# Loading the state by plain DMA in three parts, the last one gated, and batch 0 by plain DMA and casts on the engines, with a reordered instruction table

## The chip, the cores and the metric

The kernel runs on one core of a Trainium2 chip. Its inputs and outputs lie in HBM in f32. The metric is the time of one execution on the device in microseconds; smaller is better. Every experiment ran on the same chip as runs of the kernel before, in the same rounds; the sets of experiments ran on different chips, so that across sets the ratios to the kernel before are the safer comparison. A run counts as slow when it is over 1.5% above the fastest of the same kernel; the verdicts use the other runs, called fast, alone.

## The reference, cut to what matters

```python
# x: (8 batches, 8 heads, 512 tokens, 64), state: (8, 8, 32, 64)
a     = softmax(x @ state^T / 8)          # tokens read the state
xread = a @ state
a2    = softmax(state @ x^T / 8)          # the state reads the tokens
sread = a2 @ x
y     = concat([xread, sread], axis=2)    # (8, 8, 544, 64) -> (8, 544, 512)
# mixer: wq = y @ w_q, wk = y @ w_k, W = wq . wk^T / 8
out   = relu(W^T @ y) @ w_out             # (8, 544, 512)
```

The eight batches are independent of each other. All of them need the state; the weights and the state are small (1.25 MB with w_out, 0.5 MB), x and the output are 8.4 and 8.9 MB.

## The kernel before

The program is a list of steps in the variable ORDER, such as `xT0.1.t`: the step, its batch, and the engine that does it (t TensorE, v VectorE, a ScalarE, p GpSimd). Each engine executes its own steps strictly in this order. The first steps bring the data in:

```python
    for t in range(2):                     # w_q on SyncE's queue, w_k on ScalarE's
        for r in range(2):
            eng = nc.sync if t == 0 else nc.scalar
            eng.dma_start(out=w_f[64 * r : 64 * r + 64, :, t, :], in_=wsrc[t][r])
    ...
    def load(n, b, e):
        if n == "ist":                     # the whole state, cast to bf16 by GpSimd's DMA
            nc.gpsimd.dma_start(out=st_in, in_=state.rearrange(...))
            make_identity(nc, ident)
        elif n == "iwo":                   # w_out, cast on the way
            nc.gpsimd.dma_start(out=w_o, in_=moe_w_out.rearrange("(k p) e -> p k e", p=128))
        elif n[2] == "0":                  # batch 0 in two halves, cast on the way
            ...
        else:                              # batches 1 to 7, cast on the way
            nc.gpsimd.dma_start(out=x_bf[b], in_=xsrc(b, 0, H))
    ...
    def st_tr(n, b, e):                    # 64 transposes of 64x64: state to stT
    def st_back(n, b, e):                  # 16 transposes back: stT to st_bf (head layout)
    def stbd_blk(n, b, e):                 # block-diagonal state of batches 0 to 2, on GpSimd
    def stbd_dma(n, b, e):                 # the same of batches 3 to 7, by four DMAs
    ...
    def pt_mm(n, b, e):                    # scores: x^T times stT
    def srd(n, b, e):                      # 64 small matmuls of 32 columns: a2 @ x
    def mixs_mm(n, b, e):                  # 4 matmuls: the state rows of the mixer
    def fin_mm(n, b, e):                   # 4 matmuls of 512 columns: times w_out
```

All loads of x and w_out go through one queue, GpSimd's, one after the other; I call them the batch stream.

The softmax here doesn't subtract the row's maximum and nothing guards it: scores larger than these inputs give would overflow.

## Time and profile before

| | before |
|---|---|
| time, first three runs | 98.1 us median (95.94 to 99.06) |
| span of the profiled run | 95.1 us |
| TensorE busy | 81.4 us (86%) |
| TensorE's waits for a batch | 4.7 us, three times, longest 2.3 |
| last batch landed | at about 32 us |

### The profile page before, as it was taken

To read this page: it belongs to the slowest core of one execution; us is meant where nothing else is said; L and a number is where in the kernel's file an instruction comes from. 1 tells how busy PE (TensorE), PEld (TensorE's weight loads), DVE (VectorE), ACT (ScalarE), POOL (GpSimd) and SP (SyncE) were. 2 spreads that over 40 slices of the span, in tenths; PEclk is the share of its full clock that TensorE was granted. 3 is DMA by queue.
4 is the path that set the end of the run, shared out by engine and by line. 5 is a ranking of instruction groups with operands and counts; after the bars stand their busy time and mean duration, and the time that the engine had idled before them with its cause. 6 is when DMAs were issued, how large, how long until landed. Compare 5 with 4: busy or idle time off the path is not lost.

```text
span 95.1 us, 3128 instructions
## 1 busy us (share of the span) xinstructions
PE 81.4 (86%) x1376; PEld 54.3 (57%) x1376; DVE 57.3 (60%) x108; ACT 50.5 (53%) x78; POOL 38.5 (40%) x50
## 2 busy tenths in 40 slices
PE   5852898918999999999999999999999999999300
PEld 4542796806897855865875678478655544344000
DVE  3946267833385959926899689196942647637000
ACT  0507467970738994525762679468496430542400
POOL 5999609999402900290008999006113000000000
PEclk9995559995569999999999999999999999999995
DMA  0999999999999130545410253016302634762990
GB/s 6 177 153 158 194 200 205 196 200 196 198 198 145 28 52 29 234 184 215 171 62 7 110 214 127 0 45 258 148 10 58 266 124 186 324 259 48 341 352 22
DMA packets 14245, 14.51 MB, mean 153 GB/s; under 512 B 2904, under 2 KB 11608, under 8 KB 14232
## 3 DMA queue, kind: packets, MB, share of 16 engines
q0 software_dynamic: 8944, 4.98, 38.4%
q1 hardware_dynamic: 4312, 8.42, 23.8%
q10 hardware_dynamic: 976, 0.92, 2.8%
q8 instruction: 10, 0.16, 0.6%
q14 instruction: 3, 0.02, 0.1%
HBM read 10.22 MB, written 8.91 MB: 201 GB/s over the span
## 4 chain that ended last, share of the span: by engine, by line
PE 68%; DMA 16%; POOL 5%; ACT 2%; issue 2%; ACTq 1%; POOLq 0%
PE fin_ps L537 28%; DMA x_bf<-in_x_dram 16%; PE xT_ps L245 5%; PE mix_ps L503 5%; PE at_ps L321 4%; PE wq_ps L397 3%; PE pt_ps L263 3%; PE wk_ps L435 3%; PE g_ps L451 3%; PE v_ps L467 2%; PE srd_ps L334 2%; PE fins_ps L537 2%; ACT ost L128 2%; POOL x_bf L153 2%; PE v_ps L476 2%
## 5 line engine op out<-in xcount | busy, mean ns | idle before, releaser
L537 PE MATMUL fin_ps<-w_o,rmix 128*128 128x512 bf16 x128 | 30.2, 379 | 0.0
L308 POOL TENSOR_TENSOR A<-E,rinv 128x1024 bf16<-128x1024 bf16 (+1 forms) x9 | 15.4, 1720 | 22.9 <-DVE rinv L302 15.1
L537 PEld LDWEIGHTS <-rmix 128*128 128x128 bf16 x128 | 11.5, 98 | 12.0 <-issue 0.4
L245 PE MATMUL xT_ps<-ident,x_bf 128*128 128x128 bf16 x128 | 11.2, 245 | 4.7 <-DMA x_bf<-in_x_dram 4.7
L130 DVE COPY ost<-fin_ps 128x1024 f32<-128x1024 f32 (+1 forms) x9 | 10.4, 1164 | 6.0 <-PE fin_ps L537 4.5
L371 POOL TENSOR_TENSOR sbd<-srn,mask 128x256 bf16<-128x256 bf16 x16 | 9.4, 614 | 9.4 <-DVE srn L361 9.4
L128 ACT COPY ost<-fin_ps 128x1024 f32<-128x1024 f32 (+1 forms) x9 | 7.8, 871 | 9.3 <-PE fin_ps L537 8.7
L134 ACT ACTIVATE rmix<-mix_ps 128x1024 bf16<-128x1024 f32 x11 | 11.3, 1028 | 2.7 <-PE mix_ps L503 2.6
L279 ACT ACTIVATE E<-pt_ps 128x512 bf16<-128x512 f32 x16 | 9.5, 600 | 5.5 <-PE pt_ps L263 5.5
L245 PEld LDWEIGHTS <-x_bf 128*128 128x128 bf16 x128 | 8.9, 111 | 5.5 <-DMA x_bf<-in_x_dram 5.4
L294 DVE TENSOR_REDUCE rsum<-E 128x16 f32<-128x512 bf16 x16 | 10.6, 670 | 0.0
L128 ACT COPY xT<-xT_ps 128x1024 bf16<-128x1024 bf16 x8 | 8.2, 1019 | 2.3 <-PE xT_ps L245 2.3
L130 DVE COPY xT<-xT_ps 128x1024 bf16<-128x1024 bf16 x8 | 5.4, 681 | 4.3 <-PE xT_ps L245 4.2
L263 PE MATMUL pt_ps<-stT,xT 128*128 128x64 bf16 x128 | 7.1, 205 | 0.0
L130 DVE COPY AT<-at_ps 128x1024 bf16<-128x1024 bf16 x6 | 4.1, 690 | 4.7 <-PE at_ps L321 4.7
L136 DVE TENSOR_SCALAR rmix<-mix_ps 128x1024 bf16<-128x1024 f32 x5 | 6.1, 1221 | 1.0 <-PE mix_ps L503 0.9
L263 PEld LDWEIGHTS <-xT 128*128 128x128 bf16 x128 | 5.9, 106 | 0.8
L153 POOL DMA_DIRECT2D x_bf<-in_x_dram x7 | 6.2, 917 | 0.4 <-DMA x_bf<-in_x_dram 0.4
L503 PE MATMUL mix_ps<-wq,V 64*128 64x256 bf16 x64 | 5.9, 273 | 0.0
L321 PE MATMUL at_ps<-ident,A 128*128 128x128 bf16 x64 | 5.5, 231 | 0.0
L321 PEld LDWEIGHTS <-A 128*128 128x128 bf16 x64 | 4.2, 104 | 0.7 <-issue 0.4
L128 ACT CAST wq<-wq_ps 128x288 bf16<-128x288 f32 x6 | 2.4, 400 | 4.0 <-PE wq_ps L406 4.0
(75 smaller groups left out, 116.0 us busy)
## 6 DMA issues: line engine op xcount, KB each, us to landing
out_dram<-ost SPq DMA_DIRECT2D x14, 512.0 KB, 2.8
x_bf<-in_x_dram POOLq DMA_DIRECT2D x7, 512.0 KB, 17.1
out_dram<-ost SPq DMA_DIRECT2D x3, 256.0 KB, 4.7
out_dram<-ost ACTq DMA_DIRECT2D x3, 256.0 KB, 4.2
x_bf<-in_x_dram POOLq DMA_DIRECT2D x2, 256.0 KB, 6.6
w_o<-in_moe_w_out_dram POOLq DMA_DIRECT2D x1, 512.0 KB, 13.3
st_in<-in_state_dram POOLq DMA_DIRECT2D x1, 256.0 KB, 4.3
stbd<-st_bf SPq DMA_DIRECT2D x4, 40.0 KB, 2.1
```

Of the source, the lines that this page charges most:

```text
L128: nc.scalar.copy(out=out, in_=in_)
L130: nc.vector.tensor_copy(out=out, in_=in_)
L134: nc.scalar.activation(out=out, in_=in_, func=AF.Relu)
L245: nc.tensor.transpose(out=ps[:, u, q, :], in_=x_bf[b][:, NP * r + q, 128 * u : 128 * u + 128], identity=ident,)
L263: nc.tensor.matmul(out=ps[:, 2 * u : 2 * u + 2, NS * q : NS * q + NS], lhsT=L[b][f"xTe{r}"][:, u, q, :], rhs=stT[:, b, :, NP * r + q, :], ...
L279: nc.scalar.activation(out=L[b]["E"][:, r].rearrange("p c q n -> p c (q n)"), in_=L[b][f"pt{r}"], func=AF.Exp, scale=float(scale),)
L294: nc.vector.reduce_sum(out=L[b]["rsum"][:, w], in_=L[b]["E"].rearrange("p r c q n -> p (r c q) n")[:, w], axis=AX.X,)
L308: eng.tensor_tensor(out=L[b]["A"].rearrange("p r c q n -> p (r c q) n")[:, w], in0=L[b]["E"].rearrange("p r c q n -> p (r c q) n")[:, w], ...
L321: nc.tensor.transpose(out=L[b]["at"][:, r, c, :], in_=L[b]["A"][:, r, c, :, :], identity=ident)
L371: nc.gpsimd.tensor_tensor(out=L[b]["sbd"][:, r], in0=L[b]["srn"][:, r : r + 1, :].to_broadcast((128, NP, D)), in1=mask[:, :, None].to_broa ...
L503: nc.tensor.matmul(out=ps[:, h, kk, :], lhsT=L[b]["V"][rows, 128 * k : 128 * k + 128], rhs=L[b]["wq"][rows, 0:SH], start=True, stop=True,)
L537: nc.tensor.matmul(out=ps, lhsT=lhs(k), rhs=w_o[:, k, :], start=(k == 0), stop=(k == KC - 1))
```

## The change

The intent is to start TensorE's real work sooner and to free GpSimd. The state comes by plain DMA, directly in the layout that st_bf needs, in parts for batch 0, batch 1, and batches 2 to 7. The third part is gated: it is issued only after a one-column fill on GpSimd that stands behind the first batch's normalising. Batch 0 comes by four plain DMAs on two queues and is cast by three engines. The block-diagonal state is made by eight small DMAs instead of GpSimd's products, and two zero fills move from VectorE to GpSimd. The table follows the expected landings.

```diff
+    def load_st(b0, b1):
+        nc.sync.dma_start(
+            out=st_f[:, b0:b1].rearrange("p b r d -> p (b r) d"), in_=st_src[:, 2 * b0 : 2 * b1]
+        )
+    load_st(0, 1)
+    for g in range(4):
+        eng = nc.sync if g % 2 == 0 else nc.scalar
+        eng.dma_start(out=x_f0[:, 2 * g : 2 * g + 2], in_=xsrc(0, 2 * g, 2 * g + 2))
+    load_st(1, 2)
...  (the four weight loads, all on SyncE now)
-        if n == "ist":  ...                      (whole state by casting DMA)
-        elif n[2] == "0":  ...                   (batch 0 by casting DMA)
+    def st_gate(n, g, e):
+        nc.gpsimd.memset(st_f[:, 2, 0, 0:1], 0.0)
+        load_st(2, B)
+    def st_cast(n, g, e):                        # f32 to bf16
+    def st_tr(n, g, e):                          # 32 transposes of 128x64 in four groups
-    def st_back ... stb_ev ... stbd_blk          (removed)
     def stbd_dma(n, g, e):                       # now for batches 0-1 and 2-7
...  (table, cut to the place that matters)
+swe.0.a xT0.1.t srn.0.v A1.0.p at0.0.t xTe0.1.v srT.0.t xT1.1.t srTe.0.a xTe1.1.a pt0.1.t gate.10.p
+ix4.0.p at1.0.t ate.0.v exp0.1.a pt1.1.t ix5.0.p stc.2.v wq.0.t exp1.1.a rs0.1.v stt.2.t ix6.0.p
```

## The prediction

> **What bounds the kernel now.** I read the page first: the busy shares, the 40 slices, and the chain that ended last.
>
> ```profile
> PE 81.4 (86%) x1376; PEld 54.3 (57%) x1376; DVE 57.3 (60%) x108; ACT 50.5 (53%) x78; POOL 38.5 (40%) x50
> ...
> PE   5852898918999999999999999999999999999300
> ...
> PEclk9995559995569999999999999999999999999995
> DMA  0999999999999130545410253016302634762990
> ...
> PE 68%; DMA 16%; POOL 5%; ACT 2%; issue 2%; ACTq 1%; POOLq 0%
> ```
>
> A slice is 2.38 us. From slice 10 on TensorE is full until the tail, so the last 65 us can only shrink with TensorE's work or its clock. The first ten slices are different: holes, and a granted clock of 0.5 in two stretches, while the DMA engines are full until slice 12. The chain in order of time names what holds the start:
>
> ```profile
> 4.04 1.76 POOL x_bf L153 x2
> 5.80 0.71 POOL w_o L147
> 6.51 15.25 DMA x_bf<-in_x_dram
> 21.80 1.04 PE xT_ps L245 x8
> ```
>
> The load of batch 3, issued at 6.51 us, lands at 21.8 us, and TensorE waits for it. The stretches (columns: stretch, length, busy time of PE, PEld, DVE, ACT, POOL, then clock, DMA share, GB/s) give the price:
>
> ```profile
> 8.84:14.30 5.46, 5.14 (x62) 4.70 (x63) 2.31 (x5) 3.12 (x4) 2.11 (x3) 0.51 1.42 190
> 14.30:21.80 7.50, 4.78 (x184) 3.79 (x181) 4.64 (x12) 5.83 (x9) 7.22 (x9) 0.95 1.38 200
> 21.80:28.30 6.50, 6.50 (x115) 5.55 (x116) 3.70 (x7) 2.50 (x5) 3.02 (x6) 0.53 1.46 198
> 28.30:89.00 60.70, 60.48 (x943) 36.97 (x939) 40.94 (x74) 35.95 (x56) 18.39 (x19) 1.00 0.39 135
> ```
>
> Up to 21.8 us TensorE idles 0.32 + 2.72 us; then, full, it runs at 0.53 for 6.5 us, which costs about 6.5 x 0.47 = 3.1 us; after that there is no hole. So three things are to be won: an earlier first transpose (now 8.84 us), the 2.3 us wait at 21.8, and the 3.1 us of slow clock that follow. The waits name the first as well:
>
> ```profile
> 8.84 0.77 PEld L245 LDWEIGHTS <-x_bf 128*128 128x128 bf16 x8 [2.15 <-DMA x_bf<-in_x_dram]
> 10.19 0.77 PEld L245 LDWEIGHTS <-x_bf 128*128 128x128 bf16 x8 [0.57 <-DMA x_bf<-in_x_dram]
> 21.80 0.77 PEld L245 LDWEIGHTS <-x_bf 128*128 128x128 bf16 x8 [2.48 <-DMA x_bf<-in_x_dram]
> ```
>
> **What the Trainium skill says.** "TensorE: Matmul & The Clock Gate", section "Why this matters for your kernels", asks for no TensorE gaps over about 3 us, or the clock halves. The trace agrees in kind, with a shorter gap: 2.3 us without work before 21.8 us, and 0.53 granted after it. "DMA: Bandwidth & Descriptors", section "Issuing engines are not separate DMA queues", says that DMAs of all issuers share the same 16 engines and interleave. The trace agrees: the first 64 KB weight load on ScalarE's queue moves its 272 packets between 2.0 and 3.0 us, the second, issued 0.7 us after the first, only between 4.0 and 5.5 us, with the state load on GpSimd's queue between them; landing goes from 3.2 to as much as 4.4 us. The same page, "Specifications", gives 512 B as the smallest piece at full rate. Here SyncE's queue took 9.7% of 16 engines over 6 us for 544 packets of mostly 256 B, 17 ns each; no run shows yet what they cost among larger ones.
>
> **The change, part by part.**
>
> Start. Now state, then batch 0, go through GpSimd's queue and land at 5.6, 8.84 and 10.2 us. In the new kernel SyncE issues a 64 KB state part, then batch 0 comes in four 256 KB pieces on two queues. Issues take 0.80 us on SyncE, so the first piece of SyncE leaves at about 1.55 us; with the 3.2 us of an early weight load and 0.6 us for its bytes it lands near 5.4 us. It is then cast by GpSimd, which first makes the identity (0.23 + 0.29 us) and fills two 128x2048 f32 tiles that VectorE filled before (1.76 and 1.12 us). No row shows such a fill on GpSimd; its fills of 1 and 128 columns take 0.10 and 0.23 us, 1.0 ns a column, so I estimate 2.1 us each. 1.25 + 0.6 + 4.2 = 6.05 us, and the cast is 0.61 us (as w_qk's): first transpose at 6.7 us, **2.1 us earlier**.
>
> TensorE's work. Gone: 64 small state transposes (1.2 us, beside a load) and 16 back transposes (1.03 us, on the path). New: 32 transposes of 64x128, four before the start; of the other 28, 24 stand at one place, an estimate of 1.0 us at full clock from the 19 ns apiece that 64 of half the width took. In total no gain worth naming.
>
> GpSimd. Six products for the diagonal state go (6 x 0.61 = 3.7 us), replaced by eight plain DMAs of 128 B rows; those of before landed 2.1 us after issue, long before v needs them. Beside the path, except that normalising batch 0 comes sooner: now A ends 18.13 - 8.84 = 9.3 us after the first transpose, of which w_qk's cast and two products (1.8 us), and parts of the back transpose (about 0.7 us), go. So about 6.8 us remain: 6.7 + 6.8 = 13.5 us.
>
> Batches. Batches 1, 2, 3 are issued from 6.7 us on, w_o after them. Landings stood 2.63 us apart late in the stream (24.4 to 32.3 us), about 2 us behind their bytes: 12, 15 and 17.6 us (now up to 12.9, 16.6, 21.8), w_o 20.5. But the queue starts 4 us later, so batches 4 to 7 gain about 0.5 us only. **The wait at 21.8 us is gone**: batch 3 comes 4 us sooner.
>
> New wait. The third state part (batches 2 to 7, 1536 rows of 256 B, 96 an engine) is issued only after that 13.5 us, and VectorE's and TensorE's tables put its cast and transposes right behind pt of batch 1 and wq of batch 0, which I expect at 16.3 us. In-order engines stop there until it has landed. Issue to landing: 3.2 us for 16 rows an engine, plus 80 x 17 ns = 1.4 us if nothing interferes: 18.1 us, 18.6 with the cast (estimate 0.5). If each row also waits for one batch row (2.63 us x 16 / 1024 = 41 ns), 96 x 41 ns = 3.9 us more: 22.5 us.
>
> What a stop is worth: at that point the new kernel still has, against the old one at 21.8 us, srd and sums of batch 1 (0.63), three groups of xT and pt of batch 2 (0.9 + 0.23), two sw groups (0.4), srT (0.06), 24 state transposes (1.0), less wq (0.34): 2.9 us at full clock, single values from the chain's pieces. So resuming at 18.9 us is the break-even, if the clock falls there as it does now.
>
> **Rivals, and what each makes of the time.** The baseline is the mean of the four times of before, (99.06 + 95.94 + 98.1 + 97.07) / 4 = 97.5 us.
> A: the state lands before about 17 us. For: the table is said to be reordered to landings, and batch 2's transposes stand behind the state's, so its author saw the state land first; GpSimd's fills may be quicker than my line of two points, which moves everything forward. Then at most 0.7 us idle, no second slow stretch: about -1 to -2 us from the break-even and -3.1 of clock, say -4: 93.5 us.
> B: it lands at 18 to 19 us. For: the 17 ns of lone rows. Old wait replaced by a new one of the same size, same slow clock: 0, 97.5 us.
> C: rows alternate with the batch stream. For: the delayed weight loads, and the two state DMAs for the diagonal that stand before it on the queue. 21 to 22.5 us: about +2.7, 100.2 us.
> A fourth, that all is hidden by TensorE being full from slice 10 on, I discount: a hole in front moves the whole full stretch. The tail (fewer batches finished early, four finishing together) may move it by 1 us either way; 24.8 of the last 25 us of TensorE were full, so there is more to lose than to gain.
>
> **Range and chances.** 0.40 x 93.5 + 0.35 x 97.5 + 0.25 x 100.2 = 96.6 us. A gives faster (0.40), B same (0.35), C slower (0.25). The range is A's less 0.8 to C's plus 0.1, as the three runs of before alone spread over 3.1 us: 92.7 to 100.3 us.
>
> **What would show it.** Right: the first transposes of x at 6 to 7 us; no wait of TensorE for batches 1 to 3 beyond 12.5 us; A of batch 0 over at 13 to 14 us; if slower or equal, a wait of VectorE for the state's DMA in its third cast, a TensorE hole behind wq of batch 0, and clock 0.5 after it. Wrong: a first transpose after 8 us (fills or first pieces slower than I think), a TensorE wait for batch 1 of over 1 us, or holes after 35 us, which would mean the new table, not the loads, decides.

## More of the kernel before

Every matmul and every transpose is two instructions of TensorE: a load of weights and the multiplication.

The page's slices, chain and first stretches stand in the prediction. Two more views matter later. The list of waits (columns: who waited, for whom, then us in total, times, longest), and busy time by stretch (stretch, length, busy time and count of PE, PEld, DVE, ACT, POOL, then granted clock, DMA share, GB/s):

```profile
PE xT_ps L245 <- DMA x_bf<-in_x_dram: 4.7, 3, 2.3
```

```profile
20.00:26.00 6.00, 4.20 (x70) 3.48 (x71) 1.59 (x3) 2.61 (x6) 4.82 (x9) 0.59 1.46 198
...
32.00:90.00 58.00, 56.77 (x847) 34.05 (x843) 38.38 (x67) 33.22 (x52) 16.66 (x16) 1.00 0.38 141
```

The reader is to keep the last line: at 32 us TensorE has 847 matmuls (up to 90 us) still to do and is nearly full from there on. Where another kernel stands at 32 us, measured by this count, tells how much its front part won or lost.

## The result and the profile after

| | before | after |
|---|---|---|
| time, four runs each | 97.2 us median (95.94 to 99.06) | 103.22 us median (103.04 to 103.59) |
| ratio | 1 | 1.074 (1.068 to 1.081) |
| span of the profiled run | 95.1 us | 101.3 us |
| TensorE busy | 81.4 us | 80.7 us |

A ratio is the mean time of one kernel's fast runs over that of the other's of the same rounds, so it is not quite the ratio of the medians. The kernel became 7% slower; the prediction had ended its range at 100.3 us. The slices of the page after:

```profile
PE   5749795000699799999999999999999999999500
...
PEclk9995555555558999999999999999999999999996
DMA  0999999999999500014502255017650237517980
```

A slice is 2.53 us here. TensorE does nothing at all in slices 7 to 9 (counted from 0), while the DMA engines are full. The timeline (start, length, engine, line, operation, tiles, shapes, count, and in brackets the idle time before it and what ended it) shows the start of the work and the two ends of the hole:

```profile
5.98 0.62 PE L247 MATMUL xT_ps<-ident,x_bf 128*128 128x128 bf16 x8 [0.75 <-POOL x_bf L163]
...
26.22 0.85 PE L188 MATMUL stT_ps<-ident,st_bf 128*64 128x128 bf16 x12 [9.38 <-DVE st_bf L144]
```

```profile
25.60 0.56 DVE L144 CAST st_bf<-st_f 128x768 bf16<-128x768 f32 x1 [9.65 <-DMA st_f<-in_state_dram]
```

The first transpose of x came at 5.98 us, 2.9 us earlier than before. But TensorE then stood 9.4 us in front of the transposes of the third state part, because VectorE stood 9.65 us in front of its cast, because the DMA had not landed. The list of DMA issues (last column: us from issue to landing) and the chain in order of time agree:

```profile
st_f<-in_state_dram SPq DMA_DIRECT2D x1, 384.0 KB, 12.5
```

```profile
13.04 12.47 DMA st_f<-in_state_dram
25.60 0.57 DVE st_bf L144
26.22 0.85 PE stT_ps L188 x12
```

The packets by queue between 18 and 19 us show why it took so long (q0 is GpSimd's queue with the batch stream, q1 the queue of SyncE; packets, MB, share of 16 engines):

```profile
q0 software_dynamic: 157, 0.15, 90.0%
q1 hardware_dynamic: 159, 0.04, 30.7%
```

The two queues take turns, one packet each. In every microsecond from 18 to 24 us the two counts differ by three at most (155 and 154, 162 and 164, 233 and 234, 238 and 235, 239 and 239). A small row of 256 B waits for one row of the stream each time. Where w_out's larger rows pass (1 KB each, by the packet sizes in the trace), a pair takes 16 engines / 157 per us = 102 ns; where x's rows pass (0.5 KB) it takes 16 / 239 = 67 ns. The 1,536 rows of the part are 96 an engine; all but a few stragglers (the first at 16.65, the last at 25.15 us) moved from about 16.9 to 24.6 us, 7.7 us, that is 80 ns a pair.

At 32 us the front has cost this much:

```profile
20.00:26.00 6.00, 0.00 (x0) 0.00 (x0) 0.40 (x1) 0.00 (x0) 0.00 (x0) 0.50 1.35 188
...
32.00:90.00 58.00, 57.15 (x997) 37.74 (x997) 40.11 (x72) 39.22 (x65) 19.32 (x19) 1.00 0.35 118
```

The kernel after has 150 matmuls more to do by then (997 against 847; its end lies later than 90 us too), and needs 101.3 - 32 = 69.3 us to its end where the kernel before needs 63.1. So the whole loss of 6.2 us was made before 32 us.

### The profile page after: what moved, and what is told of

It is laid out like the page before. It is cut to its first block, busy times and chain, and to the rows that moved or that the text cites. A ratio compares the mean times of both kernels' runs of the same rounds, so it can differ in the third digit from the quotient of the medians.

```text
span 101.3 us, 3046 instructions
## 1 busy us (share of the span) xinstructions
PE 80.7 (80%) x1328; PEld 54.6 (54%) x1328; DVE 54.8 (54%) x107; ACT 52.5 (52%) x86; POOL 37.4 (37%) x46
## 3 DMA queue, kind: packets, MB, share of 16 engines
q0 software_dynamic: 7808, 4.19, 30.5%
q1 hardware_dynamic: 8184, 9.44, 30.1%
## 4 chain that ended last, share of the span: by engine, by line
PE 65%; DMA 17%; ACT 4%; DVE 3%; POOL 2%; issue 2%; SPq 1%; ACTq 0%; DVEq 0%; POOLq 0%
PE fin_ps L539 26%; DMA st_f<-in_state_dram 12%; PE xT_ps L247 7%; DMA x_f<-in_x_dram 5%; PE mix_ps L505 4%; PE pt_ps L265 3%; PE at_ps L323 3%; PE wk_ps L437 3%; PE srd_ps L336 3%; PE v_ps L469 2%; ACT ost L142 2%; PE g_ps L453 2%; PE wq_ps L399 2%; PE stT_ps L188 2%; POOL A L310 2%; PE fins_ps L539 2%
## 5 line engine op out<-in xcount | busy, mean ns | idle before, releaser
L142 ACT COPY ost<-fin_ps 128x1024 f32<-128x1024 f32 (+1 forms) x11 | 9.4, 863 | 12.1 <-PE fin_ps L539 7.1
L144 DVE COPY ost<-fin_ps 128x1024 f32<-128x1024 f32 x7 | 8.6, 1223 | 8.6 <-PE fin_ps L539 8.6
L188 PE MATMUL stT_ps<-ident,st_bf 128*64 128x128 bf16 x32 | 2.4, 303 | 10.0 <-DVE st_bf L144 10.0
L150 DVE TENSOR_SCALAR rmix<-mix_ps 128x1024 bf16<-128x1024 f32 x7 | 8.4, 1214 | 3.1 <-PE mix_ps L505 3.0
L148 ACT ACTIVATE rmix<-mix_ps 128x1024 bf16<-128x1024 f32 x9 | 9.1, 1022 | 0.6 <-ACT ost L142 0.4
L144 DVE CAST st_bf<-st_f 128x128 bf16<-128x128 f32 (+1 forms) x3 | 2.4, 797 | 11.8 <-DMA st_f<-in_state_dram 11.8
L142 ACT COPY xT<-xT_ps 128x1024 bf16<-128x1024 bf16 x7 | 7.1, 1017 | 2.9 <-PE xT_ps L247 2.8
L142 ACT COPY stT<-stT_ps 64x256 bf16<-64x256 bf16 (+1 forms) x4 | 2.3, 577 | 11.5 <-PE stT_ps L188 11.4
L144 DVE COPY xT<-xT_ps 128x1024 bf16<-128x1024 bf16 x9 | 6.2, 689 | 3.7 <-PE xT_ps L247 3.6
L188 PEld LDWEIGHTS <-st_bf 128*64 128x64 bf16 x32 | 1.6, 157 | 10.6 <-DVE st_bf L144 10.6
## 6 DMA issues: line engine op xcount, KB each, us to landing
x_bf<-in_x_dram POOLq DMA_DIRECT2D x7, 512.0 KB, 13.5
st_f<-in_state_dram SPq DMA_DIRECT2D x1, 384.0 KB, 12.5
```

The costliest lines, as they stand in the source:

```text
L142: nc.scalar.copy(out=out, in_=in_)
L144: nc.vector.tensor_copy(out=out, in_=in_)
L148: nc.scalar.activation(out=out, in_=in_, func=AF.Relu)
L150: nc.vector.tensor_scalar(out=out, in0=in_, scalar1=0.0, scalar2=None, op0=ALU.max)
```

## The experiments

My theory after this result: the hole is the landing of the third part, late through the alternation with the batch stream; without the hole the kernel gains what the prediction's case A said, about 4 us. Rivals: the loss is in the slow clock (TensorE's granted clock stood at 0.5 from 7.2 us to about 31 us in this profile); in the order of queues; in the place in the table; or the gain of the earlier start is not there to be had. All times below are of the kernel after with the edit shown. Results were correct unless said otherwise.

**The third part early.** It is issued without the gate, ahead of the weights.

```diff
     load_st(1, 2)
+    load_st(2, B)
...
     def st_gate(n, g, e):
-        nc.gpsimd.memset(st_f[:, 2, 0, 0:1], 0.0)
-        load_st(2, B)
+        pass
```

> The changed kernel with one move: the third state part is issued at the start, behind the second one, and its gate is gone; the table is untouched. Theory (the late landing of that part makes the whole loss): it lands before 10 us, the 9.4 us hole of TensorE behind wq of batch 0 goes, and about 1 to 3 us of slow clock with it: 103.2 - 9.4 - 1 = 91 to 94 us, faster than the kernel before. Rival (the new table and its tail, or the plain loads of batch 0, cost the time, and the hole only hides them): 98 us or more, with new holes of TensorE after 30 us.

Measured: 98.98 us median (97.41 to 100.61), ratio 1.008 (0.993 to 1.024). The part landed 5.7 us after its issue and the 9.4 us hole was gone. So the gated load made the loss of 6 us. But there was no gain over the kernel before either. The weights of w_k stood behind the part now, and GpSimd, then TensorE, waited for them (timeline; this profile fell on a slow run, so I read the wait from it and no time):

```profile
14.20 0.42 PE L226 MATMUL sw_ps<-w_qk,stT 64*32 64x128 bf16 x16 [3.48 <-POOL w_qk L217]
```

**The hole filled.** TensorE does 60 matmuls on zeros in front of the transposes of the third part, so that its clock does not fall; they write PSUM tiles that nobody reads.

```diff
     def st_tr(n, g, e):
         b0, b1 = SGR[g]
+        if g == 2:
+            for i in range(10):
+                wp = psA.tile([128, 2, 512], FP, name="fill_ps", tag="psA")
+                for j in range(6):
+                    nc.tensor.matmul(out=wp[:, j % 2, 0:256], lhsT=zero[:, 0:128], rhs=zero, ...)
```

> The changed kernel with 60 matmuls on zeros ahead of the third part's transposes, so that TensorE is busy while it waits. The landing is not touched. If the slow clock after the hole costs 2 to 3 us of its own: the clock is 1.0 at 26 to 31 us instead of 0.5 and the time falls to 100.5 to 101.5 us. If the wait alone counts (work after it limited by the other engines): 103 us, no change.

Measured: 102.78 us median (101.57 to 103.85), ratio 1.054 (1.041 to 1.068). The clock was 1.0 from about 18 us on, yet of the 6 us only 0.4 (by the medians, 103.22 - 102.78) to 1.9 came back (by the ratios, 0.020 x 97). The slow clock behind the hole is a small part of the loss. The four runs of the kernel after say it without an experiment: all are fast, their mean granted clocks were 0.873, 0.987, 0.894 and 0.938, and they took 103.13, 103.32, 103.59 and 103.04 us. The run that had nearly the full clock was no faster. One line of its timeline was strange, and I come back to it:

```profile
34.92 0.22 PE L270 MATMUL pt_ps<-stT,xT 128*128 128x64 bf16 x2 [0.81 <-issue]
```

**The gate ahead of the diagonal's DMAs.** The four DMAs for the diagonal of batches 0 and 1 stood ahead of the third part on SyncE's queue; here they stand behind it.

```diff
-pt1.0.t exp1.0.a sg.0.p rs0.0.v ... pt0.1.t gate.10.p ix4.0.p
+pt1.0.t exp1.0.a rs0.0.v ... pt0.1.t gate.10.p sg.0.p ix4.0.p
```

> The changed kernel with the first diagonal group (four plain DMAs of 128 B rows) issued behind the gated third part instead of ahead of it, on the same queue. If the queue's order counts (the state rows stand behind 544 packets of the diagonal): data starts 2 us sooner, landing about 10 us after issue instead of 12.5, time about 100 to 101 us. If the one to one turn with the batch stream is all: landing stays at 12 us or more and the time at 103 us.

Measured: 102.68 us median (102.38 to 102.92), ratio 1.057 (1.049 to 1.066). The part landed 12.2 us after issue instead of 12.5, and the hole stayed:

```profile
25.85 0.85 PE L188 MATMUL stT_ps<-ident,st_bf 128*64 128x128 bf16 x12 [9.24 <-DVE st_bf L144]
```

In both kernels the part's own packets begin at about 16.9 us. The order on SyncE's queue is not the cause. This run also tells what the slow clock ahead of the hole is worth: its clock was about 0.9 or more up to the hole, against 0.5 from about 7 us on in the kernel after, and it ended only 0.5 us sooner by the medians, 1.6 by the ratios.

**The table waits later (overshot).** All steps that use the third part (cast, transposes, their copies, sw of batches 2 to 7, the scores of batch 2) were moved far back in the table, behind other work of batches 0 and 1; the loads stayed.

```diff
-... ix5.0.p stc.2.v wq.0.t exp1.1.a rs0.1.v stt.2.t ix6.0.p wks.0.t stt.3.t stf.2.a ...
+... ix5.0.p wq.0.t exp1.1.a rs0.1.v ix6.0.p wks.0.t ...  (the block follows far later)
```

> The changed kernel with the loads untouched; only the table differs: the third part's cast and transposes come after all work of batches 0 and 1 that does not need them and after the x transposes of batches 2 and 3. Theory (the loss is an in-order wait, not the load): the part still lands at 24 to 26 us, TensorE fills the hole with about 8 us of work, and the time falls by 6 to 9 us, to 94 to 97 us. Rival (loads as such slow the kernel through contention): 101 us or more.

Measured: 108.27 us median (106.39 to 109.27), ratio 1.101 (1.084 to 1.117). VectorE came to the cast only at 37.1 us, about 11 us after the landing, and batches 2 and 3 starved. The edit went past its aim and tells nothing about the theories.

**The table waits somewhat later.** The same block, now right behind wke of batch 1.

```diff
-... ix5.0.p stc.2.v wq.0.t exp1.1.a rs0.1.v stt.2.t ix6.0.p wks.0.t ...
+... ix5.0.p wq.0.t exp1.1.a rs0.1.v ix6.0.p wks.0.t ...
+... wqe.1.a wke.1.v stc.2.v stt.2.t stt.3.t stf.2.a ste.3.v ...
```

> The first try put the third part's cast behind eight more steps than needed (VectorE reached it only at 37 us). Here it comes behind wk of batch 1, where TensorE is at about 25.5 us. Theory: loads as in the changed kernel, landing near 26 us, TensorE waits 2 us or less for it and the clock stays up: 96 to 99 us. Rival (no order of work helps, since batches 2 and 3 starve later): over 101 us.

Measured: 102.06 us median (101.88 to 102.19), ratio 1.055 (1.049 to 1.061). The hole shrank from 9.4 to 3.1 us, but only 1.2 us were gained by the medians, 1.9 by the ratios:

```profile
26.73 1.49 PE L180 MATMUL stT_ps<-ident,st_bf 128*64 128x128 bf16 x24 [3.07 <-DVE st_bf L136]
```

That work drawn forward into the hole is missing later is my reading; no run tests it. Of the two orders that I tried, neither mended the late landing.

**The third part behind the weights.** As the first experiment, but ungated behind the four weight loads, so that nothing waits for w_k.

```diff
             nc.sync.dma_start(out=w_f[64 * r : 64 * r + 64, :, t, :], in_=wsrc[t][r])
+    load_st(2, B)
...
-        nc.gpsimd.memset(st_f[:, 2, 0, 0:1], 0.0)
-        load_st(2, B)
+        pass
```

> As the run with the third part at the start, but issued behind the four weight loads, so that it can't hold them up. Theory (there the hole was only exchanged for a 3.5 us wait for the weights, and 4 us of stops in the instruction stream): the wait for w_qk goes, the third part lands at 12 to 14 us, before its cast at about 16, and the time falls to 94.5 to 96 us, with stops of 1 to 2.5 us left at TensorE's instruction rows 702 and 958, the same rows as before. Rival (start is bound by the batch stream whatever the order): no better than the 97.4 to 98.4 us of that run's fast executions.

Measured: 97.92 us median (96.57 to 99.22), ratio 1.0 (0.990 to 1.010). Everything that case A asked for is there: the first transpose at 5.93 us, the third part ready, the clock at 1.0. And yet it is equal to the kernel before. The timeline has three waits of over a microsecond:

```profile
13.58 1.03 PE L247 MATMUL xT_ps<-ident,x_bf 128*128 128x128 bf16 x8 [2.23 <-DMA x_bf<-in_x_dram]
...
25.63 0.17 PE L525 MATMUL mixs_ps<-wq,V 64*128 64x32 bf16 x1 [1.59 <-issue]
...
31.84 0.24 PE L336 MATMUL srd_ps<-x_bf,E 128*32 128x64 bf16 x6 [2.45 <-issue]
```

Batch 1 landed 1.6 us later than in the kernel after (its transposes began at 13.58 against 11.95 us), probably because the small rows alternate with it now. And two stops of 4.0 us together wait for "issue": nothing that the profile shows held TensorE. In the middle of a step of four matmuls it stopped, and in the middle of a step of 64.

Between its first transpose and 32 us, TensorE idled 7.2 us here and 3.0 us in the kernel before:

```profile
8.84:32.00 23.16, 20.12 (x453) 16.97 (x454) 13.20 (x30) 14.66 (x25) 14.09 (x21) 0.74 1.32 183
5.93:32.00 26.07, 18.84 (x464) 15.16 (x464) 15.47 (x34) 15.21 (x26) 16.05 (x19) 1.00 1.43 195
```

The first line is the kernel before. The 4.2 us of added idle time, less 1.3 us of busy time (the clock was full here, 0.74 there), are the 2.9 us of the earlier start. Of the 7.2 us, 4.0 are the two stops and 2.2 the wait for batch 1.

The stops have a pattern. Counted in the trace (and in the compiled program), the first falls at instruction 702 of TensorE, the second at 958: 256 apart. In the run with the hole filled, 120 instructions were put in ahead of that place, and its stop fell on quite another matmul (pt) but again on instruction 958. The kernel after itself stops 0.58 us at 702, the run with the gate ahead 0.57 us, the run with the third part early 1.56 and 2.45 us at both, and the run whose table waits somewhat later 1.33 us at 958, one record sooner. So it is the place in the stream of instructions that counts, and not the operation. The DMA view has a small queue of its own for them, here between 29.0 and 29.5 us:

```profile
q8 instruction: 1, 0.02, 11.8%
```

The page counts 10 such packets, 0.16 MB: 16 KB each. TensorE has 2,656 loads and multiplications, 10.4 times 256. In this run the packets pass in the half microseconds from 14.0, 23.0, 29.0 and 33.0 us: each of the two stops lies just behind one and ends about 2.5 us after its start. Over all traces there are 20 such stops of 0.25 us or more, and each ends 1.2 to 1.6 us after the end of a packet of this queue: TensorE goes on when the block is there.

How long a block takes can be read too. While the batch stream runs, a block's packet starts 3.5, 3.6 and 3.8 us after TensorE has entered the 256 instructions ahead of it (at 10.81, 19.58 and 25.63 us); the next one, just behind the stream's end, 1.6 us after (31.84 to 33.45 us). The third state part's own first row came as late in the kernel after, 3.6 us after its issue. From TensorE's restart behind the first stop (25.63 us) to its restart behind the second (31.84 us) are 6.2 us, of which the 256 instructions took 3.8 at full clock; the rest is the second stop. My theory changed here: while the stream runs, TensorE gets 256 instructions every 6 us or so, and an earlier start is given back at these places. The stretch at 32 us says the same:

```profile
32.00:90.00 58.00, 56.75 (x850) 35.59 (x844) 37.02 (x63) 35.05 (x57) 16.45 (x17) 1.00 0.38 140
```

850 matmuls to go, 847 in the kernel before: the start of 2.9 us has been used up.

**Batch 0 by the casting load.** The previous kernel, with batch 0 by two casting DMAs on GpSimd's queue as in the kernel before, and no casts on the engines.

```diff
-    for g in range(4):
-        eng = nc.sync if g % 2 == 0 else nc.scalar
-        eng.dma_start(out=x_f0[:, 2 * g : 2 * g + 2], in_=xsrc(0, 2 * g, 2 * g + 2))
...
+    load_st(2, B)
     make_identity(nc, ident)
+    for h0 in (0, NP):
+        nc.gpsimd.dma_start(out=x_bf[0][:, h0 : h0 + NP], in_=xsrc(0, h0, h0 + NP))
```

> As e7_third_behind_weights, with batch 0 loaded as before, by two casting DMAs of GpSimd's queue, and no engine casts. If the plain loads of batch 0 are worth the 2.9 us that the first transpose came earlier: first transposes at 8 to 9 us and 2 to 3 us slower than e7. If an earlier start is eaten up later by the stops of the instruction stream and the batch stream: equal to e7 within 1 us.

Measured: 97.66 us median (97.11 to 98.99), ratio 1.009 (1.000 to 1.019), within 1% of the run with the plain loads (1.0). The first transpose of x came at 7.17 instead of 5.93 us, but the transposes of batch 1 began at 13.52 against 13.58 us, and the two stops were there (1.12 and 2.42 us). Batch 0's faster way wins 1.2 us at the start and less than a per cent, within the noise, at the end.

**The stream cut short (a wrong result).** The kernel with the third part behind the weights, without the loads of batches 6 and 7; they use batch 5's tile.

```diff
-    x_bf = [const.tile([128, H, NC * D], BF, name=f"x_bf{b}") for b in range(B)]
+    x_bf = [const.tile([128, H, NC * D], BF, name=f"x_bf{b}") for b in range(6)]
+    x_bf += [x_bf[5], x_bf[5]]
...  (ix6.0.p and ix7.0.p taken from the table)
```

> As e7_third_behind_weights, but batches 6 and 7 are not loaded and compute on batch 5's tile (a wrong result on purpose). The batch stream ends near 25 us instead of 31. Theory (the instruction fetch of TensorE is slow only behind the batch stream): the stop at row 958 (near 27 to 30 us) goes, that at row 702 stays; 1 to 2.5 us faster than e7. Rival (the stops have another cause, such as a block that TensorE simply outruns): both stay, and the time is equal to e7 within 0.7 us.

Measured: 94.91 us median of four; the one fast run took 93.46 us, against 96.57 and 96.93 of the kernel with all loads. The slices of DMA fall off at about 27 us instead of 31. The stop at instruction 702 stayed:

```profile
24.34 0.17 PE L518 MATMUL mixs_ps<-wq,V 64*128 64x32 bf16 x1 [1.30 <-issue]
...
28.34 0.24 PE L329 MATMUL srd_ps<-x_bf,E 128*32 128x64 bf16 x6 [0.25 <-issue]
```

The stop at 958 shrank from 2.45 to 0.25 us; its block had come 3.8 us after the one before it (25.97 against 22.14 us), where the run with all loads has 6.2 us. That is what the fetch theory expects of a stream that ends sooner, though the stream's last packet passed only at 27.2 us, 1.3 us behind that block. One caution: less data to load also makes batch loads cheaper in other ways, and only one run was fast, so the 3 us are no exact price of the stop.

**The third part on the stream's own queue.** It is issued by GpSimd directly behind batch 1, where it comes in turn and cannot alternate with the stream.

```diff
             nc.gpsimd.dma_start(out=x_bf[b], in_=xsrc(b, 0, H))
+            if b == 1:
+                nc.gpsimd.dma_start(
+                    out=st_f[:, 2:B].rearrange("p b r d -> p (b r) d"), in_=st_src[:, 4 : 2 * B]
+                )
...
-        nc.gpsimd.memset(st_f[:, 2, 0, 0:1], 0.0)
-        load_st(2, B)
+        pass
```

> The third state part is issued without a gate on the queue that carries the batches, directly behind batch 1, so that it doesn't alternate with them but comes in turn; the weights stay where the changed kernel has them. If the landing was late because its small rows alternate with the batch stream: it lands within 6 us of its issue, by about 15 us, before its cast is due at 16; TensorE waits for no DMA over 1.5 us, the batch behind it comes about 1 to 2 us later than in the run with the load behind the weights, and the issue stops at rows 702 and 958 stay, so that the time is 95.5 to 98 us, equal to the kernel before within 2%. Rival (1,536 small rows are slow on any queue while the stream runs): landing more than 9 us after issue, a wait of TensorE of over 3 us in front of the transposes of the state, and over 99 us.

Measured: 96.93 us median (95.01 to 97.54, two of six runs fast), ratio 0.985 (0.975 to 0.995). It was run again in fresh rounds:

> The run with the third part on the batches' queue again, in fresh rounds, because its first verdict rests on two fast runs. If the gain is real: a ratio of 0.98 to 0.99 to the kernel before, 95 to 96.5 us in fast runs, with the third part landing in 6 to 7 us and the stops at rows 702 and 958 in the trace. Rival (the two fast runs were lucky): 0.995 to 1.005.

Measured: 96.84 us median (96.1 to 97.12, all six fast), ratio 0.999 (0.990 to 1.008). The rival of that run was right: the 1.5% did not repeat. From the second run's trace, the list of issues and the timeline:

```profile
st_f<-in_state_dram POOLq DMA_DIRECT2D x1, 384.0 KB, 6.8
```

```profile
12.48 0.62 PE L250 MATMUL xT_ps<-ident,x_bf 128*128 128x128 bf16 x8 [0.60 <-DMA x_bf<-in_x_dram]
...
23.82 0.17 PE L528 MATMUL mixs_ps<-wq,V 64*128 64x32 bf16 x1 [1.38 <-issue]
...
30.02 0.24 PE L339 MATMUL srd_ps<-x_bf,E 128*32 128x64 bf16 x6 [2.44 <-issue]
```

The part landed in 6.8 us, with the stream running, and before its cast was due. TensorE lost 0.6 us to a batch and 3.8 us to the two stops, and the time was that of the kernel before again. The queue is not the only thing that differs, though. The page counts 15,685 packets here and 17,124 where the part is on SyncE's queue. On GpSimd's queue the count rose by 112 (7,920 against 7,808), where the other fell by 1,552. The packet sizes in the trace show the same: besides 16 ends of the transfer, the part went in 96 packets of 4 KB instead of 1,536 of 256 B. So this run shows that the landing can be quick, and not how much of that is the turn and how much the larger packets.

**The stream started sooner.** As the run before, with batch 1 and the third part issued ahead of GpSimd's zero fill for the diagonal and its first cast.

```diff
-zst.0.p zbd.0.p stc.0.v ... xc0.0.p xc1.0.a ix1.0.p xT0.0.t ... iwo.0.p exp0.0.a
+zst.0.p ix1.0.p stc.0.v ... xc0.0.p xc1.0.a xT0.0.t ... iwo.0.p zbd.0.p exp0.0.a
```

> As the run before, but batch 1 and the third state part are issued ahead of the zero fill of the diagonal state and of the first cast, which stands behind w_o's issue now: the stream starts about 1.5 to 2 us sooner. If the front is bound by the stream (the fetches of TensorE's instructions are slow for as long as it runs): the stream ends 1.5 to 2 us sooner, the stop at row 958 is shorter or gone, and the time is 1 to 2 us under the run before, 94 to 96.5 us. Rival (the stream ends when it did, since its later parts are issued behind GpSimd's work): the same stops, and the time equal to the run before within 0.5 us.

Measured: 98.45 us median (97.08 to 100.27), ratio 1.007 (0.998 to 1.015). Batch 1 was issued at 3.0 us instead of 6.1, but the plain loads that run beside the stream came later: the second group of transposes of batch 0 began at 8.20 us, against 7.14 in the run with the third part behind the weights that shared its rounds. The stops stayed. Its timeline:

```profile
8.20 1.13 PE L242 MATMUL xT_ps<-ident,x_bf 128*128 128x128 bf16 x8 [1.23 <-DVE x_bf L136]
...
10.55 0.43 PE L183 MATMUL stT_ps<-ident,st_bf 128*64 128x128 bf16 x4 [1.21 <-DVE st_bf L136]
...
25.60 0.17 PE L520 MATMUL mixs_ps<-wq,V 64*128 64x32 bf16 x1 [1.30 <-issue]
...
31.80 0.24 PE L331 MATMUL srd_ps<-x_bf,E 128*32 128x64 bf16 x6 [2.44 <-issue]
```

My expectation of 1 to 2 us fell; the rival's "same stops" was right. Its "equal to the run before" was not: the run before it is the one with the third part on the stream's queue, 1.5% under the kernel before in the same rounds (0.1% in its second set), and this one is 0.7% over it. In this trace, what was saved at one load was lost at another.

**The third part behind the weights, again**, in the rounds of the last two for comparison.

> The run with the third part behind the weights again, in the same rounds as the two others: equal to the kernel before within 1%, 96.5 to 98 us, with stops of TensorE at program rows 702 and 958 of 1.3 to 2.5 us. If the place of the third part on the batches' queue is better, it is 0.5 to 1.5 us slower than that run; the rival says equal.

Measured: 98.56 us median (96.63 to 98.9), with one fast run of six, 96.63 us; its profile fell on a slow run. It gives no ratio. The stops of 1.4 and 2.4 us were there. By fast runs, the place on the stream's queue (second run, 96.1 to 97.1 us) is neither shown better nor worse than this one.

Whether any of these versions beats the kernel before by more than a per cent is not shown. None does so in two sets of runs.

## Why the prediction was wrong

By its own steps:

- **The start: right, and a bit better.** Predicted 2.1 us earlier, measured 2.9 (5.98 against 8.84 us). GpSimd's fills took 1.80 us each where I estimated 2.1.
- **The gate: right.** Predicted 13.5 us, measured 12.93 for the fill, and 13.04 for the issue.
- **Batches: right for their order.** The transposes of batch 1 began at 11.95 us, for a predicted landing of 12; the wait of TensorE for a batch was 0.56 us, within the limit of 1 us that I had set.
- **The new wait: right in kind, its size wrong. This is the step that failed.** "Issue to landing: 3.2 us for 16 rows an engine, plus 80 x 17 ns" was case B; with "each row also waits for one batch row ... 41 ns" it became case C, 13.5 + 3.2 + 1.4 + 3.9 = 22.0 us, a time of 8.5 us from issue to landing. Measured were 12.5. The mechanism is that of C: the packets of the two queues alternate one to one. The terms were mis-sized: a pair took 80 ns on the average (102 beside w_out's rows, 67 beside x's) and not 17 + 41 = 58; 96 pairs make 7.7 us where I had 5.6. And what lies ahead of the first row and behind the last was 3.9 + 0.9 = 4.8 us; I had taken 8.5 - 5.6 = 2.9 from an early load with little else in flight. I had forgotten that w_out's larger rows, which I myself had put behind batch 3, would pass just then.
- **What a stop is worth: about right.** The break-even was a restart at 18.9 us. It came at 26.22, 7.3 us later, which would give 97.5 + 7.3 = 104.8 us; measured 103.2. The signs named for a slower kernel all came: VectorE's wait in its third cast (9.65 us), the hole behind wq of batch 0, and clock 0.5 after it. One small thing: the baseline of 97.5 is the mean of slow and fast runs; the fast ones took 95.9 to 97.1 us.
- **The chances: wrong through this.** I gave the late landing 0.25 although the profile before had shown the weight loads delayed by alternation, and set the end of the range from its mis-sized terms.
- **Case A, the gain: wrong, and this the result alone does not show.** "A hole in front moves the whole full stretch", with 4 us to be won, of which 3.1 from the clock, and "at most 0.7 us idle". The runs with the third part behind the weights and on the stream's queue have no such hole, have the early start, and end where the kernel before ends. The rival that I discounted, that the gain is hidden on the way, was right in its outcome, though not for its reason (that TensorE is full from slice 10 on): in the run with the third part behind the weights TensorE idled 7.2 us up to 32 us, 4.0 of them for its own instructions, which come in blocks of 256, about 6 us apart while the batch stream runs. And the 3.1 us of clock do not show either: among the fast runs of the kernel before, those with a mean granted clock under 0.94 took 96.3 to 97.45 us (six runs), those over 0.975 took 96.41 to 98.11 us (five); with the slow runs the means are 97.9 (fifteen runs) and 97.7 us (ten).

  In the kernel before the same blocks pass at 20.3, 26.5 and 30.2 us and no stop over 0.3 us waits for one: TensorE takes 6.6 us (a wait for a batch in it) and then 5.4 us (at half clock) for the 256 instructions ahead of places 702 and 958, so that the blocks are there in time. That the half clock only hides what a stop would cost otherwise fits these numbers; it is argued, not shown.

What stays open: the exact share of the stops in the gain that did not come (the trace has them where they must lie, and one run without most of the later stop was about 3 us faster, but that run loaded less as well, and I had no way to fetch instructions otherwise); what makes a fetch slow beside the stream; and how much of the third part's late landing is the turn with the stream and how much its small packets, which no run separates.

"Runtime: NRT & Kernel Launch", section "Instruction fetch mechanics", says that the instructions come through a FIFO in 16 KiB blocks of 256, on a DMA queue of the sequencer's own, and that the cost of a boundary is "mostly hidden". The trace agrees with the blocks and the queue; hidden the cost was not in the runs with the early start, at up to 2.45 us a boundary.

## What to carry to other kernels

Small rows on a second queue beside a running stream should be priced per pair of packets, by the stream's row size at that very time, and not by what they cost alone; put them ahead of the stream or in its queue. An in-order table that names a late load early turns that lateness into a stop of every engine. And before paying for an earlier start, look at what else paces the front: where TensorE stops for "issue" at places 256 instructions apart, its instruction stream may be the limit, and loading sooner won nothing here.

## What the Trainium skill lacked or had wrong

- "Runtime: NRT & Kernel Launch", section "Instruction fetch mechanics", calls the cost of a block boundary mostly hidden. Beside a batch stream that keeps the DMA engines full, TensorE stopped 0.8 to 1.6 us at instruction 702 and 2.4 us at 958 in the runs without the hole; the page has no number for a fetch beside the kernel's own loads (here the packet started 3.5 to 3.8 us after the block ahead was entered, and 1.6 us just behind the stream).
- "DMA: Bandwidth & Descriptors", section "Queues, rings and completion order", has each engine drain a packet of typically 9 to 17 descriptors before it turns to the next queue. In the profile's records the two queues alternate one small row to one row of the stream (157 to 159 and 239 to 239 packets in a microsecond); whether such a record is a packet in the page's sense no run shows.
- The same page, "Specifications", names 512 B as the least size for full rate, but no price beside a stream: 256 B rows cost 67 to 102 ns a pair there.
- The same page, "SWDGE vs HWDGE vs iDMA", gives a packet of GpSimd's way as at best 4,096 B, which the trace agrees with, but has no such figure for SyncE's on this chip: the same plain load of 256 B rows made 112 records on GpSimd's queue and 1,552 on SyncE's, differences of the profiles' counts (7,920 - 7,808 and 8,184 - 6,632).
- "TensorE: Matmul & The Clock Gate", section "Why this matters for your kernels", warns of gaps of over about 3 us for the fall of the clock. The profiled run of the kernel after stood at 0.5 from about 7 us on, behind gaps of 0.6 to 0.8 us only, while the first run with the third part behind the weights kept 1.0 through a wait of 2.2 us, and the same kernel's second profile fell to 0.5 at about 8 us behind gaps no longer than 0.7 us. The four runs of the kernel after had mean clocks from 0.873 to 0.987. So gaps alone do not decide it here; what does, no run shows.
